# Two column tiles in one bank for the half-size group of the last layer's first product, and every other row store of the group before from GpSimd

## The chip, the core and the metric

The kernel runs on one core of one Trainium2 chip. The metric is the device time of one execution in microseconds (us); where several runs are given, it is their median. The program uses five engines that run side by side: PE (matrix products, with PEld for its weight loads), DVE (element-wise work, 32x32 transposes), ACT (copies and activations), POOL (GpSimd) and SP (which here issues DMAs). They wait for each other through semaphores. Products accumulate in PSUM banks of 128 partitions by 512 fp32 values.

## The reference

Three layers follow one another; all data are fp32.

```python
def reference(q, k, v, moe..., moe2...):
    x = attention(q, k, v)            # 8 batches x 8 heads, 576 rows, softmax inside chunks of 64
    x = x.reshape(4608, 512)
    x = ((x @ w1) * (x @ w2)) @ w3 @ w_out          # moe: 512 -> 1024 -> 512
    h = x @ w_in                                    # moe2: 512 -> 2048
    g = np.maximum(h, 0) + alpha * np.minimum(h, 0) # one alpha for each of the 2048 columns
    return g @ w_out2                               # 2048 -> 512
```

Only the last layer, moe2, is touched by the change.

## The kernel before

**Precision.** An fp32 operand is held as two parts, a rounded high part and the remainder. A product of two operands is three matmuls (PASSES: high·low, high·high, low·high), and a product over 256 values of the inner dimension is six matmuls ("x6" in the rows).

**moe2 in groups.** The 4608 tokens are nine blocks of 512 (TB). Both products of moe2 are computed in a Strassen-like way, as seven products of sums of quadrants in place of eight of the quadrants. Four groups (s = 0 to 3) take two blocks each; the fifth (s = 4) takes the one block left over and splits it in two halves of 256 tokens. That is `wide = [512, 512, 512, 512, 256]`: a matmul of a wide group has 512 columns, one of the half-size group 256.

**First product** (lines 595 to 651). The loop at line 610 goes over the groups and, in each, over the eight column tiles j of the hidden layer, two at a time (`jj`). One turn of that loop is called a pass here: four for each group, 20 in all. A pass has 14 steps of six matmuls: products 4 of both tiles into the banks `a` and `b`, product 5 of the first tile into one bank of a pair called `bc`, 3, 5, then 0, 2, 6 and 1. The pairs `bc` rotate over three places (`att`, `p01`, `p23`). ACT copies `a` and `b` after products 4, 3 and 0 into temporaries named p1, u2 and v (`keep`, L619; rows shorten the names to p, u, v); DVE adds the banks of `bc` to them (`add`, L441). `leaky` (L601 to L608) takes a finished quadrant: ACT forms relu(h) (L605, into a new tile `r`) and relu(-h) (L606), DVE joins the two with alpha (L607), and SP stores `r` to DRAM (L608, `g_dram<-r`). All the temporaries, r, t, p1, u2, v and the later `o` too, come from one pool of seven buffers of 128 x 512 fp32 (`tmp`, TMP = 7), also where only 256 columns are used. A buffer of `r` is free when its store has landed.

**Second product** (lines 724 to 800). Each group reads its quadrants back (`raw`, L678: `araw<-g_dram`, four slots, fetched three ahead on SP), splits them or their sums into two parts (`spread`: ACT casts at L658, DVE subtracts at L441), and multiplies. A group has three loops over m = 0 to 3; the first multiplies by two operands into the banks `a`, `b` and `q`, the second by three, the third by two. The results lie in a tile `post`. Those of a wide group are written out while the next group is in its first loop: `rows` (L710 to L721) is called eight times for a group; each call has DVE transpose 32x32 pieces of `post` into a tile `o` (L716) and then issues four stores of 64 KB (L720, `out<-o 32x4x128`), so 32 stores for a group. The half-size group, the last, has `turned` in its place (L696 to L708), which transposes on PE.

**What sets the order.** A scheduler puts the instructions of each engine in order; on PE the order of the code is kept through the whole of moe2. Each engine works through its queue in order, so an instruction that waits holds up all behind it on that engine. SP issues every DMA of the kernel before; POOL issues none. While the half-size group is in its first product, SP also fetches the second product's weights into places that come free (`weights`, L431).

Of the kernel before, what the change touches and what calls it, by code (L numbers as in the profile page):

```python
# [14 lines left out]
ALU = mybir.AluOpType  # L15
# [3 lines left out]
P = 128  # L19
TB = 512  # L20
# [47 lines left out]
def tile_attention_moe_moe(ctx: ExitStack, tc: tile.TileContext, qkv: bass.AP, w12: bass.AP,  # L68
# [54 lines left out]
    def tmp(name):  # L123
        return work.tile([P, TB], F32, tag="tmp", name=name, bufs=TMP)
# [9 lines left out]
    def bank(which):  # L134
        return psum.tile([P, TB], F32, tag=which, name=which, bufs=1)
# [459 lines left out]
    def product(s, j, o, ps, first, last):  # L595
# [3 lines left out]
                       start=first and k + i == 0, stop=k == 1 and i == 2, skip_group_check=not (first and last))  # L599
        if j == NJ - 1 and s + 1 < len(wide):  # L600
            operand(o)  # L601
    def leaky(s, j, q, h, t):
        w, f = wide[s], j + NJ * (q % 2)
        r = tmp("r")[:, :w]
        nc.scalar.activation(out=r, in_=h, func=AF.Relu)  # L605
        nc.scalar.activation(out=t, in_=h, func=AF.Relu, scale=-1.0)  # L606
        nc.vector.scalar_tensor_tensor(out=r, in0=t, scalar=nalpha[:, f:f + 1], in1=r, op0=ALU.mult, op1=ALU.add)  # L607
        nc.sync.dma_start(out=g2_dram[s, q, j // 2][:, j % 2], in_=r)  # L608

    for s, j in [(s, j) for s in range(len(wide)) for j in range(0, NJ, 2)]:  # L610
        w, jj = wide[s], (j, j + 1)
        if j == 2 and s + 1 < len(wide):
            load_y(s + 1)
        a = [bank(n)[:, :w] for n in "ab"]
        p1, u2, v, b, c = ([None] * 2 for _ in range(5))

        def keep(name, i):
            t = tmp(name)[:, :w]
            nc.scalar.copy(t, a[i])  # L619
            return t  # L620

        def second(i):
            n = 4 * NJ * s + j + i
            bc = pair(("att", "p01", "p23")[n % 3], "bc")
            b[i], c[i] = (bc[:, h, :w] for h in range(2))
            product(s, jj[i], 5, b[i], True, True)
            add(p1[i], p1[i], b[i])
            leaky(s, jj[i], 0, p1[i], p1[i])

        for i in range(2):  # L630
            product(s, jj[i], 4, a[i], True, False)
            p1[i] = keep("p1", i)
        second(0)
        for i in range(2):
            product(s, jj[i], 3, a[i], False, False)
            u2[i] = keep("u2", i)
        second(1)
        for i in range(2):
            product(s, jj[i], 0, a[i], False, False)
            v[i] = keep("v", i)  # L640
        for i in range(2):
            product(s, jj[i], 2, c[i], True, False)
            add(v[i], v[i], c[i])
            leaky(s, jj[i], 3, v[i], v[i])
        for i in range(2):
            product(s, jj[i], 6, a[i], False, True)
            leaky(s, jj[i], 1, a[i], tmp("t")[:, :w])
        for i in range(2):
            product(s, jj[i], 1, c[i], False, True)
            add(u2[i], u2[i], c[i])  # L650
            leaky(s, jj[i], 2, u2[i], u2[i])

# [57 lines left out]
    def rows(s, quads, half, t):  # L710

        w = wide[s]
        o = tmp("o")
        ob = o.rearrange("p (b h e c) -> p h e b c", b=4, h=2, e=2)
        for h, c in enumerate(quads):
            nc.vector.transpose(ob[:, h], c[:, :, t * P:(t + 1) * P].rearrange("p e (b c) -> p e b c", c=32))  # L716
        b, r = (PAIRS[s][half], 0) if w == TB else (0, half * w)
        r += b * TB + t * P
        for a in range(4):
            nc.sync.dma_start(out=out[r:r + P, a * P:(a + 1) * P].rearrange("(b r) c -> r b c", r=32),  # L720
                              in_=o[a * 32:(a + 1) * 32].rearrange("p (b c) -> p b c", c=P))  # L721

    x_t.pop("w")
# [124 lines left out]
```

## Time and profile before

| what | us |
|---|---|
| median of three runs | 1462.27 |
| lowest and highest of them | 1460.94 and 1463.52 |
| the profiled execution's own time | 1463.75 |
| its span, from the first to the last instruction | 1461.9 |
| PE busy in the span | 1411.9 |
| first product of moe2, four wide groups | 743.00 to 1054.98 |
| first product, half-size group | 1054.98 to 1105.42 |
| second product, four wide groups | 1105.42 to 1410.63 |
| second product, half-size group | 1410.63 to 1455.31 |

The stretches are cut where PE begins with a stage. The granted TensorE clock over the span was 0.995 of full speed. In the rows, a tile's name before the arrow is what is written, behind it what is read; "x6" is the number of instructions put together; "us" behind the start is their busy time. Matmuls overlap, so a group's busy time is longer than the time to the next group's start; the step from start to start is what counts.

### The profile page before, as it was taken

How to read it: one execution, taken by the hardware profiler on the slowest of the kernel's cores; microseconds unless marked ns; L12 is line 12 of the kernel's file. 1: busy time of each engine (PE TensorE's matmuls, PEld its weight loads, DVE VectorE, ACT ScalarE, POOL GpSimd, SP SyncE). 2: the span in 40 equal slices, each digit the busy share in tenths (PEclk: the TensorE clock that was granted, in tenths of full speed). 3: DMA queues.
4: the chain of work that ended last, by engine and by line, in shares of the span. 5: the costliest groups of instructions: out<-in, count | busy, mean ns of one | idle time of the engine just before them, and what ended most of it. 6: DMA issues, size and time to landing. Idle time of an engine off the chain costs nothing.

```text
span 1461.9 us, 22936 instructions
## 1 busy us (share of the span) xinstructions
PE 1411.9 (97%) x8608; PEld 1167.7 (80%) x8608; DVE 1001.7 (69%) x1533; ACT 737.5 (50%) x1603; POOL 0.7 (0%) x6
## 2 busy tenths in 40 slices
PE   4999999999999999999999999999999999999998
PEld 3777788887788888888878787878787888888887
DVE  4988786233487877776345758575756878888775
ACT  5545532144355545553247767686765444444433
POOL 0000000000000000000000000000000000000000
PEclk9999999999999999999999999999999999999999
DMA  8555342344466666668272424333589563745442
GB/s 260 188 188 168 108 157 95 131 151 148 141 216 217 216 216 220 218 221 304 91 273 108 148 112 158 116 137 116 177 277 324 188 216 116 210 136 176 144 140 89
DMA packets 132095, 256.32 MB, mean 175 GB/s; under 512 B 13712, under 2 KB 62864, under 8 KB 131984
## 3 DMA queue, kind: packets, MB, share of 16 engines
q1 hardware_dynamic: 131984, 254.87, 52.0%
q8 instruction: 67, 1.10, 0.3%
q14 instruction: 44, 0.36, 0.1%
HBM read 160.44 MB, written 94.37 MB: 174 GB/s over the span
## 4 chain that ended last, share of the span: by engine, by line
PE 83%; DVE 6%; ACT 5%; DMA 4%; issue 1%; SPq 0%; ACTq 0%; DVEq 0%
PE a L109 18%; PE b L109 18%; PE q L109 17%; PE acc L109 12%; PE bc L109 8%; PE ab L109 4%; PE wc L109 3%; ACT e L303 2%; DMA g_dram<-r 2%; PE sc L109 1%; PE pa L109 1%; DMA raw<-in_w 1%; PE pa L114 1%; DVE m L181 1%; DVE m L196 1%
## 5 line engine op out<-in xcount | busy, mean ns | idle before, releaser
L109 PE MATMUL q<-op,w 128*128 128x512 f32 (+1 forms) x1020 | 220.5, 369 | 2.2 <-DVE op L441 2.1
L109 PE MATMUL acc<-gs,wc 128*128 128x512 f32 x864 | 207.9, 393 | 3.4 <-DVE gs L121 3.1
L109 PEld LDWEIGHTS q<-op,w 128*128 128x128 f32 x1020 | 179.4, 190 | 34.4 <-DVE op L441 2.6
L109 PEld LDWEIGHTS acc<-gs,wc 128*128 128x128 f32 x864 | 160.3, 188 | 40.7 <-DVE gs L121 5.2
L109 PE MATMUL a<-x,wa 128*128 128x512 f32 x672 | 165.1, 394 | 0.4 <-DVE x L342 0.4
L109 PE MATMUL b<-x,wa 128*128 128x512 f32 x672 | 163.9, 392 | 0.0
L109 PEld LDWEIGHTS a<-x,wa 128*128 128x128 f32 x672 | 127.1, 190 | 27.1 <-DVE x L342 0.5
L109 PEld LDWEIGHTS b<-x,wa 128*128 128x128 f32 x672 | 124.8, 188 | 25.8
L109 PE MATMUL bc<-yo,w 128*128 128x512 f32 (+1 forms) x600 | 134.6, 368 | 0.0
L658 ACT CAST op<-araw 128x1024 fp32r<-128x1024 f32 (+1 forms) x80 | 77.3, 967 | 94.4 <-PE q L109 33.1
L109 PEld LDWEIGHTS bc<-yo,w 128*128 128x128 f32 x600 | 105.5, 189 | 18.7
L109 PE MATMUL b<-yo,w 128*128 128x512 f32 (+1 forms) x450 | 105.3, 369 | 1.7 <-ACT t L606 1.4
L441 DVE TENSOR_TENSOR op<-araw,op 128x1024 fp32r<-128x1024 f32 (+1 forms) x80 | 88.8, 1112 | 21.1 <-ACT op L658 20.5
L109 PE MATMUL ab<-x,wa 128*128 128x512 f32 x384 | 96.4, 400 | 4.9 <-ACT a L507 4.9
L109 PE MATMUL a<-yo,w 128*128 128x512 f32 (+1 forms) x390 | 92.1, 372 | 7.3 <-ACT p L619 5.0
L303 ACT ACTIVATE e<-sc,mx 128x64 f32<-128x64 f32 x288 | 86.2, 351 | 21.8 <-DVE mx L292 21.0
L109 PEld LDWEIGHTS b<-yo,w 128*128 128x128 f32 x450 | 79.1, 188 | 17.4 <-ACT t L606 3.0
L658 ACT CAST op<-sum 128x1024 fp32r<-128x1024 f32 (+1 forms) x60 | 58.0, 967 | 64.8 <-PE q L109 48.2
L109 PEld LDWEIGHTS ab<-x,wa 128*128 128x128 f32 x384 | 71.5, 190 | 23.2 <-ACT a L507 8.4
L109 PEld LDWEIGHTS a<-yo,w 128*128 128x128 f32 x390 | 68.3, 188 | 23.1 <-ACT p L619 6.6
L441 DVE TENSOR_TENSOR op<-sum,op 128x1024 fp32r<-128x1024 f32 (+1 forms) x60 | 66.6, 1109 | 28.1 <-ACT op L658 28.1
L303 ACT ACTIVATION_READ_ACCUMULATOR e<-sc,mx 128x1 f32 x288 | 70.1, 244 | 0.0
(121 smaller groups left out, 2075.6 us busy)
## 6 DMA issues: line engine op xcount, KB each, us to landing
araw<-g_dram SPq DMA_DIRECT2D x80, 512.0 KB, 3.9
g_dram<-r SPq DMA_DIRECT2D x128, 256.0 KB, 2.0
w_dram<-wm SPq DMA_DIRECT2D x48, 512.0 KB, 2.9
w<-w_dram SPq DMA_DIRECT2D x48, 512.0 KB, 4.9
qk<-in_qkv SPq DMA_DIRECT2D x36, 512.0 KB, 5.8
raw<-in_w2nd SPq DMA_DIRECT2D x32, 512.0 KB, 4.2
y_dram<-y SPq DMA_DIRECT2D x36, 256.0 KB, 2.8
raw<-in_w SPq DMA_DIRECT2D x16, 512.0 KB, 4.2
```

Source lines behind the costliest of these rows:

```text
L109: ins = nc.tensor.matmul(*args, **kw)
L114: ins = nc.tensor.transpose(*args, **kw)
L181: nc.vector.scalar_tensor_tensor(out=m.bitcast(U32), in0=conv_raw[i][:, :, 1], scalar=0xC0000000, in1=m.bitcast(U32), op0=ALU.bitwise_and, ...
L196: nc.vector.tensor_tensor(out=m, in0=m, in1=g[:, HI].bitcast(F32), op=ALU.subtract)
L303: nc.scalar.activation(out=e[:, j, a, h], in_=s[:, h2, n * D:(n + 1) * D], func=AF.Exp, bias=mx[:, h2, n:n + 1], scale=SCALE, accum_out=sm ...
L441: nc.vector.tensor_tensor(out=out, in0=x, in1=y, op=op)
L658: ins = nc.scalar.copy(out, x)
```

## The change

Two things are changed. The first is in the first product. Where a matmul has 256 columns, one bank of 512 now holds two column tiles side by side: the half-size group's eight column tiles are taken in two passes of four, two tiles to a bank, in place of four passes of two. Every step then is twelve matmuls (`both`), and each copy, addition and activation runs once over the 512 columns of two tiles; the joining with alpha, which has one alpha for each tile, still runs once for each tile over 256 columns, and a store moves both tiles (256 KB in place of 128). Only the first tile in a bank starts it. The pair `bc` is now chosen by the count of passes. The wide groups' code comes out as before.

The second is in `rows`: for the last wide group (s = 3), whose 32 row stores are issued during the half-size group's second product, two of each four stores are issued from POOL (`nc.gpsimd`) in place of SP.

```diff
-    def leaky(s, j, q, h, t):
-        w, f = wide[s], j + NJ * (q % 2)
-        r = tmp("r")[:, :w]
+    def leaky(s, js, q, h, t):
+        w, r = wide[s], tmp("r")[:, :h.shape[1]]
         nc.scalar.activation(out=r, in_=h, func=AF.Relu)
         nc.scalar.activation(out=t, in_=h, func=AF.Relu, scale=-1.0)
-        nc.vector.scalar_tensor_tensor(out=r, in0=t, scalar=nalpha[:, f:f + 1], in1=r, op0=ALU.mult, op1=ALU.add)
-        nc.sync.dma_start(out=g2_dram[s, q, j // 2][:, j % 2], in_=r)
-
-    for s, j in [(s, j) for s in range(len(wide)) for j in range(0, NJ, 2)]:
-        w, jj = wide[s], (j, j + 1)
+        for i, j in enumerate(js):
+            f, at = j + NJ * (q % 2), slice(i * w, (i + 1) * w)
+            nc.vector.scalar_tensor_tensor(out=r[:, at], in0=t[:, at], scalar=nalpha[:, f:f + 1], in1=r[:, at],
+                                           op0=ALU.mult, op1=ALU.add)
+        j = js[0]
+        to = g2_dram[s, q, j // 2]
+        nc.sync.dma_start(out=to[:, j % 2] if len(js) == 1 else to, in_=r if len(js) == 1 else r.rearrange("p (j c) -> p j c", j=2))
+
+    passes = []
+    for s, w in enumerate(wide):
+        n = TB // w
+        passes += [(s, j, [list(range(j + i * n, j + (i + 1) * n)) for i in range(2)]) for j in range(0, NJ, 2 * n)]
+
+    for turn, (s, j, jj) in enumerate(passes):
...
+        def both(i, o, ps, first, last):
+            w = wide[s]
+            for n, k in enumerate(jj[i]):
+                product(s, k, o, ps[:, n * w:(n + 1) * w], first and n == 0, last)
...
         def second(i):
-            n = 4 * NJ * s + j + i
-            bc = pair(("att", "p01", "p23")[n % 3], "bc")
-            b[i], c[i] = (bc[:, h, :w] for h in range(2))
-            product(s, jj[i], 5, b[i], True, True)
+            bc = pair(("att", "p01", "p23")[(2 * turn + i) % 3], "bc")
+            b[i], c[i] = (bc[:, h] for h in range(2))
+            both(i, 5, b[i], True, True)
             add(p1[i], p1[i], b[i])
             leaky(s, jj[i], 0, p1[i], p1[i])
 
         for i in range(2):
-            product(s, jj[i], 4, a[i], True, False)
+            both(i, 4, a[i], True, False)
             p1[i] = keep("p1", i)
...
         for a in range(4):
-            nc.sync.dma_start(out=out[r:r + P, a * P:(a + 1) * P].rearrange("(b r) c -> r b c", r=32),
+            queue = nc.gpsimd if s == len(PAIRS) - 1 and a % 2 else nc.sync
+            queue.dma_start(out=out[r:r + P, a * P:(a + 1) * P].rearrange("(b r) c -> r b c", r=32),
                               in_=o[a * 32:(a + 1) * 32].rearrange("p (b c) -> p b c", c=P))
```

Up to the half-size group's first pass the order on every engine is the same as before. PE's queue at the start of that pass, in the kernel before (`yo` is an operand of the group, `w_...` and `wx` weights):

```order
L109 MATMUL a<-yo,w_6802 128x256 x6
L109 MATMUL b<-yo,w_6880 128x256 x6
L109 MATMUL bc<-yo,w_6802 128x256 x6
L109 MATMUL a<-yo,w_6800 128x256 x6
L109 MATMUL b<-yo,w_6878 128x256 x6
L109 MATMUL bc<-yo,w_6880 128x256 x6
```

and in the changed kernel:

```order
L109 MATMUL a<-yo,w_6802 128x256 x6
L109 MATMUL a<-yo,w_6880 128x256 x6
L109 MATMUL b<-yo,w_7213 128x256 x6
L109 MATMUL b<-yo,wx 128x256 x6
L109 MATMUL bc<-yo,w_6802 128x256 x6
L109 MATMUL bc<-yo,w_6880 128x256 x6
L109 MATMUL a<-yo,w_6800 128x256 x6
L109 MATMUL a<-yo,w_6878 128x256 x6
```

The two tiles of one product now follow each other into the same bank, so PE meets the first bank `a` again after twelve matmuls more than before. The count of matmuls is the same.

SP's queue at the change from the fourth wide group to the half-size one in the second product, before (a load's name has quadrant and m: `g_dram_0_2` is the quadrant with index 0, m = 2):

```order
L720 DMA out<-o 32x4x128 x8
L678 DMA araw<-g_dram_3_2_251 128x2x256
L720 DMA out<-o 32x4x128 x8
L678 DMA araw<-g_dram_2_3_248 128x2x256
L678 DMA araw<-g_dram_3_3_252 128x2x256
L720 DMA out<-o 32x4x128 x8
L678 DMA araw<-g_dram_0_0_237 128x2x256
L678 DMA araw<-g_dram_2_0_245 128x2x256
L720 DMA out<-o 32x4x128 x8
L678 DMA araw<-g_dram_0_1_238 128x2x256
L678 DMA araw<-g_dram_2_1_246 128x2x256
L678 DMA araw<-g_dram_0_2_239 128x2x256
```

and now:

```order
L733 DMA out<-o 32x4x128 x4
L690 DMA araw<-g_dram_3_2_251 128x2x256
L733 DMA out<-o 32x4x128 x4
L690 DMA araw<-g_dram_2_3_248 128x2x256
L690 DMA araw<-g_dram_0_0_237 128x2x256
L690 DMA araw<-g_dram_3_3_252 128x2x256
L733 DMA out<-o 32x4x128 x4
L690 DMA araw<-g_dram_2_0_245 128x2x256
L733 DMA out<-o 32x4x128 x4
L690 DMA araw<-g_dram_0_1_238 128x2x256
L690 DMA araw<-g_dram_2_1_246 128x2x256
L690 DMA araw<-g_dram_0_2_239 128x2x256
```

Each block of eight stores is one of four, the loads keep their order but for `0_0`, which stands ahead of `3_3` now, and sixteen stores have gone from this queue. They stand on POOL's, behind the few instructions of its start:

```order
masks.py:197 MEMSET ident 128x128
masks.py:199 ISA
masks.py:199 AFFINE_SELECT ident<-ident 128x128
L733 DMA out<-o 32x4x128 x16
L858 UNCONDITIONAL_BRANCH
```

DVE's queue at the same place, before (`o_12891` is the last of the group's eight tiles `o`, and `post_10369<-q` the addition that closes the fourth group):

```order
L441 TENSOR_TENSOR sum_12798<-araw_12742,araw_12744 128x2x256
L441 TENSOR_TENSOR post_10369<-q_12102,post_10369 128x1024
L441 TENSOR_TENSOR op_12753<-sum_12746,op_12752 128x2x256
L716 STREAM_TRANSPOSE o_12832<-post_10369 128x2x4x32
L441 TENSOR_TENSOR op_12801<-araw_12744,op_12800 128x2x256
L716 STREAM_TRANSPOSE o_12839<-post_10369 128x2x4x32
L716 STREAM_TRANSPOSE o_12884<-post_10369 128x2x4x32
L441 TENSOR_TENSOR op_12805<-sum_12798,op_12804 128x2x256
L716 STREAM_TRANSPOSE o_12884<-post_10369 128x2x4x32
L716 STREAM_TRANSPOSE o_12891<-post_10369 128x2x4x32 x2
L441 TENSOR_TENSOR sum_12850<-araw_12794,araw_12796 128x2x256
```

and now (`o_12779` is the last of the eight):

```order
L728 STREAM_TRANSPOSE o_12727<-post_10257 128x2x4x32
L441 TENSOR_TENSOR op_12637<-araw_12578,op_12636 128x2x256
L728 STREAM_TRANSPOSE o_12772<-post_10257 128x2x4x32
L728 STREAM_TRANSPOSE o_12779<-post_10257 128x2x4x32
L441 TENSOR_TENSOR post_10257<-q_11990,post_10257 128x1024
L441 TENSOR_TENSOR op_12641<-sum_12634,op_12640 128x2x256
L728 STREAM_TRANSPOSE o_12720<-post_10257 128x2x4x32
L441 TENSOR_TENSOR op_12689<-araw_12632,op_12688 128x2x256
L728 STREAM_TRANSPOSE o_12727<-post_10257 128x2x4x32
L441 TENSOR_TENSOR sum_12738<-araw_12682,araw_12684 128x2x256
L441 TENSOR_TENSOR op_12693<-sum_12686,op_12692 128x2x256
L728 STREAM_TRANSPOSE o_12772<-post_10257 128x2x4x32
```

The first transpose into the eighth tile has moved ahead of the closing addition; with seven buffers, it waits until the four stores of the first tile, two from SP and two from POOL, have landed.

## Rows read from the trace of the kernel before

**Rows 1.** Windows: stretch, its length, engines' busy us (instructions), granted clock, DMA share, GB/s.

```profile
743.00:1054.98 311.98, 307.14 (x1345) 251.58 (x1344) 195.75 (x262) 225.25 (x379) 0.00 (x0) 1.00 0.39 142
1054.98:1105.42 50.44, 43.96 (x337) 40.98 (x335) 30.60 (x63) 33.89 (x91) 0.00 (x0) 1.00 0.85 279
1410.63:1455.31 44.68, 42.46 (x337) 41.99 (x336) 31.05 (x52) 17.23 (x30) 0.00 (x0) 0.96 0.40 112
1430.70:1434.30 3.60, 3.60 (x18) 3.60 (x19) 2.68 (x5) 0.68 (x2) 0.00 (x0) 0.56 0.50 135
1120.00:1130.00 10.00, 10.00 (x45) 8.26 (x45) 5.22 (x6) 5.17 (x7) 0.00 (x0) 1.00 1.01 399
```

**Rows 2.** PE timeline: start, us, matmuls; wide pass, half-size stage's start and its end.

```profile
1016.90 1.52 PE L109 MATMUL a<-yo,wx 128*128 128x512 f32 x6
1018.26 1.52 PE L109 MATMUL b<-yo,w 128*128 128x512 f32 x6
...
1055.69 0.88 PE L109 MATMUL b<-yo,w 128*128 128x256 f32 x6
1056.41 0.88 PE L109 MATMUL bc<-yo,w 128*128 128x256 f32 x6
1059.23 0.98 PE L109 MATMUL a<-yo,w 128*128 128x256 f32 x6 [1.94 <-ACT p L619]
...
1105.42 0.96 PE L109 MATMUL a<-op,w 128*128 128x512 f32 x3 [1.26 <-ACT t L606]
```

**Rows 3.** What PE waited for in the half-size stage: us in total, times, longest.

```profile
PE a L109 <- ACT p L619: 3.6, 4, 1.9
```

**Rows 4.** ACT by form: one wide pass and more, then the half-size stage.

```profile
L605 ACT ACTIVATE r<-p 128x512 f32<-128x512 f32 x4 | 2.5, 632 | 5.9 <-DVE p L441 5.9
...
L619 ACT COPY p<-a 128x512 f32<-128x512 f32 x2 | 1.2, 579 | 0.0
...
L619 ACT COPY p<-a 128x256 f32<-128x256 f32 x4 | 1.4, 351 | 0.0
```

**Rows 5.** Stores of the first product: the half-size stage's, then the wide passes'.

```profile
  ACT v L619: 3.1, 4
...
DMA to landing us min/median/max: 1.7/3.5/4.6
...
DMA to landing us min/median/max: 2.0/2.0/2.9
```

**Rows 6.** SP's queue before the load that was waited for; the chain's step on it.

```profile
1400.85 5.34 SPq L720 DMA_DIRECT2D out<-o  x8
...
1416.98 1.18 SPq L678 DMA_DIRECT2D araw<-g_dram  x2
1418.26 4.01 SPq L720 DMA_DIRECT2D out<-o  x8
...
1423.65 4.97 DMA araw<-g_dram
```

**Rows 7.** DVE around that load.

```profile
1428.64 0.69 DVE L441 TENSOR_TENSOR sum<-sum,araw 128x512 f32<-128x512 f32 x1 [1.22 <-DMA araw<-g_dram]
...
1429.96 0.68 DVE L441 TENSOR_TENSOR op<-araw,op 128x512 fp32r<-128x512 f32 x1
```

**Rows 8.** PE timeline of the same stretch.

```profile
1426.87 1.70 PE L109 MATMUL q<-op,w 128*128 128x256 f32 x12
1430.70 2.59 PE L109 MATMUL q<-op,w 128*128 128x256 f32 x12 [2.12 <-DVE op L441]
...
1435.16 1.12 PE L109 MATMUL q<-op,w 128*128 128x256 f32 x8
```

**Rows 9.** DVE while the last 32 row stores are issued.

```profile
L716 DVE STREAM_TRANSPOSE o<-post 128x256 f32<-128x256 f32 x16 | 6.1, 421 | 2.4 <-ACT post L658 2.4
```

**Rows 10.** Row stores: issue to landing over all 128; the last output stores.

```profile
DMA to landing us min/median/max: 1.6/2.4/5.7
...
1457.00 1.84 SPq L708 DMA_DIRECT2D out<-o  x4
```

More of the change, by code (lines that the diff above doesn't have):

```diff
@@ L601, in product @@
             operand(o)
-    def leaky(s, j, q, h, t):
-        w, f = wide[s], j + NJ * (q % 2)
-        r = tmp("r")[:, :w]
+    def leaky(s, js, q, h, t):
+        w, r = wide[s], tmp("r")[:, :h.shape[1]]
         nc.scalar.activation(out=r, in_=h, func=AF.Relu)
         nc.scalar.activation(out=t, in_=h, func=AF.Relu, scale=-1.0)
-        nc.vector.scalar_tensor_tensor(out=r, in0=t, scalar=nalpha[:, f:f + 1], in1=r, op0=ALU.mult, op1=ALU.add)
-        nc.sync.dma_start(out=g2_dram[s, q, j // 2][:, j % 2], in_=r)
-    for s, j in [(s, j) for s in range(len(wide)) for j in range(0, NJ, 2)]:
-        w, jj = wide[s], (j, j + 1)
+        for i, j in enumerate(js):
[10 more added lines that the diff above has]
+    for turn, (s, j, jj) in enumerate(passes):
         if j == 2 and s + 1 < len(wide):
             load_y(s + 1)
-        a = [bank(n)[:, :w] for n in "ab"]
+        a = [bank(n) for n in "ab"]
         p1, u2, v, b, c = ([None] * 2 for _ in range(5))
+        def both(i, o, ps, first, last):
+            w = wide[s]
+            for n, k in enumerate(jj[i]):
+                product(s, k, o, ps[:, n * w:(n + 1) * w], first and n == 0, last)
         def keep(name, i):
-            t = tmp(name)[:, :w]
+            t = tmp(name)
             nc.scalar.copy(t, a[i])
@@ L634, in tile_attention_moe_moe @@
         for i in range(2):
-            product(s, jj[i], 3, a[i], False, False)
+            both(i, 3, a[i], False, False)
             u2[i] = keep("u2", i)
@@ L638, in tile_attention_moe_moe @@
         for i in range(2):
-            product(s, jj[i], 0, a[i], False, False)
+            both(i, 0, a[i], False, False)
             v[i] = keep("v", i)
         for i in range(2):
-            product(s, jj[i], 2, c[i], True, False)
+            both(i, 2, c[i], True, False)
             add(v[i], v[i], c[i])
@@ L645, in tile_attention_moe_moe @@
         for i in range(2):
-            product(s, jj[i], 6, a[i], False, True)
-            leaky(s, jj[i], 1, a[i], tmp("t")[:, :w])
+            both(i, 6, a[i], False, True)
+            leaky(s, jj[i], 1, a[i], tmp("t"))
         for i in range(2):
-            product(s, jj[i], 1, c[i], False, True)
+            both(i, 1, c[i], False, True)
             add(u2[i], u2[i], c[i])
```

## The prediction

> **What bounds the kernel now.** I read the table of windows first, one window for each stage of the last layer [rows 1]. In the wide groups' first product PE is busy for 307.14 of 311.98 us: it is the bound, and only more or faster matmuls would change it. In the half-size group's it is busy for 43.96 of 50.44, with ACT at 33.89, DVE at 30.60 and the DMA engines at 0.85 of their time: no engine is full, so they wait for each other. The half-size group's second product has a smaller hole, 42.46 of 44.68 at a granted clock of 0.96. The change touches these two places and nothing else in PE's work.
>
> Then PE's timeline [rows 2], for the step that a stage would keep without waits. In a wide pass six matmuls start 1.36 us after the six before (1016.90 to 1018.26); in the half-size stage 0.72 us (1055.69 to 1056.41). Fourteen steps in four passes make 56 x 0.72 = 40.32 us, and the stage takes 50.44: it loses 10.12 us. The first loss is the longest: at 1056.41 + 0.72 = 1057.13 PE was free, and it went on at 1059.23, released by ACT's copy of bank `a`: 2.10 us. The last is at its end, 1.26 us for ACT again. The view of waits puts ACT's copy p first, with 3.6 us in four waits [rows 3], once in each pass; the rest are short ones.
>
> Why ACT is late: it has 22 operations in a pass (6 copies, 16 activations), and at 256 columns these don't get shorter by half. The copy takes 351 ns at 256 columns and 579 at 512 [rows 4]. On top, ACT waits for buffers: the half-size stage's stores land after 3.5 us in the median, up to 4.6, where the wide passes' take 2.0, and ACT's v alone waits 3.1 us for such a landing [rows 5].
>
> **Part 1, two tiles to a bank.** PE's count stays at 336 matmuls of 256 columns; 40.32 us remains the floor. ACT goes from 88 operations to 44 of 512 columns, at 579 to 632 ns [rows 4]: 22 x 0.61 = 13.4 us in a pass of 28 x 0.72 = 20.16, two thirds. Before, the same engine was busy for 33.89 of 50.44 us and PE's passes would have been 10.08. The pattern is now that of a wide pass, whose steps are 1.36 us where here they are 1.44, with the same ACT operations. So the wide groups are the model: 16 passes x 14 x 1.36 = 304.64 against 311.98 us, a loss of 0.46 a pass at most, mostly the cast of the next group's operands, which the half-size group doesn't have to make. DVE keeps 32 joinings of 256 columns and halves its 24 additions: it gets shorter, and PE waited for none of its work there. SP issues 16 stores for 32, with the same bytes.
>
> Two losses stay. At the start ACT is still busy with the wide pass before: its copy of `a` ended near 1059.23 and, 0.23 us longer now, ends near 1059.46, while PE comes back to `a` after six of the old steps, at 1054.98 + 4.32 = 1059.30. That is 0.2, say 0.3 with the hop between engines. At the end the second product's first matmul must wait for the last reading of bank `a` or `b`, and that waits for a buffer of which the store has to land; the last `t` is wanted at most some 0.7 us after the pass's last matmul and comes within half a us of it with landings of 3.5 us. I take 0.4. So part 1 gives 10.12 - 0.3 - 0.4 = 9.4 us. Bounds: 10.1 if nothing stays, and half, 5.1, if landings hold ACT as they do now.
>
> **Part 2, half the row stores from POOL.** Back from the hole [rows 8]: the twelve matmuls at 1426.87 take 12 x 0.12 = 1.44, so PE was free at 1428.31 and went on at 1430.70, after DVE's op: 2.39 us. That op ran from 1429.96 [rows 7], behind a sum that waited until 1428.64 for a load. The chain gives that load: issued at 1423.65, under way for 4.97 [rows 6]. It stands behind a block of eight stores that kept SP from 1418.26 for 4.01 us [rows 6], 0.50 each. The block now has four: 2.0 us earlier, and as much again from the block before it (which delayed two loads that this chain's DVE steps also wait for); of the load's own issue I can count on some 3 us, since then its slot comes free only when DVE has used up its former content. PE needs 2.39. So it lands in time, with some 0.6 to 1 us to spare.
>
> After the hole PE ran slowly: from 1430.70 to 1435.16 it made 24 matmuls, 4.46 us in place of 2.88, in a stretch at a granted clock of 0.56 [rows 1, 8], that is near the lower of the two levels, 1.2 GHz for 2.4. The clock had been 1.00 through the half-size stage with its waits of up to 1.94 us, so that the pause of 2.39 brought it down is likely, not shown. Without the pause I take both back: 2.39 + 1.58 = 3.97 us. Bounds: 0, if another thing comes last there, and with the whole of that stage's 44.68 - 40.32 = 4.36, 4.4. Below 0 SP can't bring it: its queue only gets shorter, and the one load that moved (`0_0`) moved ahead.
>
> What POOL takes for a store no row shows. The lower bound is SP's 0.50; the upper one is 5.7, the slowest landing of a row store [rows 10], if POOL were held until each has landed. It lies nearest to SP's issue, the same act on another engine: I take 1 us. It has cover. The first of these stores is ready at 1400.85 [rows 6], the last output of the kernel is issued by 1457.00 + 1.84 = 1458.84 [rows 10]: 58 us for 16 stores, 3.6 each, before they set the end. A shorter cover is DVE's: its first transpose into the eighth tile now waits for the first tile's stores, two of them POOL's, and stands ahead of the closing addition and of two operands of PE. DVE comes there about 1411, ten us after the first store; two stores and a landing of 2.4 fit in that up to 3.8 us each. So part 2 costs nothing there at 1 us.
>
> DVE in that stretch makes 16 transposes [rows 9]; its other work there is additions and subtractions. The Trainium skill, page "SBUF — State Buffer", section "SBUF: two separate sides", speaks against this part: a DMA issued from POOL has its descriptors written by GpSimd, which is locked out while DVE runs an operation in a two-port mode, and the next section tells of a transfer that took 3.1 us in place of 0.62 next to such copies. By that, as an estimate, 16 stores at 3.1 us make 50 us, inside the cover of 58, so the sum would be the same; no run here shows a DMA from POOL.
>
> **The sum.** 9.4 + 3.97 = 13.4 us. The profiled run took 1463.75 with 1461.9 of span; the changed kernel would take 1450.35 profiled, 1448.5 of span. Against the median of 1462.27: 1448.9.
>
> **The rivals.**
> A. Part 2 gives nothing: the load is issued earlier but its slot, or DVE's order before it, comes last in its place, and the hole stays. For it: the loads rotate through four slots, and the spare time is under 1 us. Against: the 4.97 us of landing was with 32 stores in one queue. 1462.27 - 9.4 = 1452.9.
> B. Part 1 gives half: ACT waits for landings instead of its own queue. For it: DMA at 0.85 of its time, and the same bytes, 50.44 us x 279 GB/s = 14.1 MB, would have to move in 41 us, at 343 GB/s; landings get longer. Against: 399 GB/s is reached from 1120 to 1130 [rows 1], and a buffer has twice the time until it is wanted. 1462.27 - 5.1 - 4.0 = 1453.2. A and B both: 1457.2.
> C. The stage ends earlier, but the second product's first groups then wait for their weights and loads, that come through DMA engines already full there (1.01 of their time from 1120 to 1130 [rows 1]); up to all of part 1 is given back: 1458.3. With part 2 lost too: 1462.3, no change.
> D, the slower side. POOL takes more than 3.6 us for a store, so that its sixteenth comes after all else. Slower than before it is from (58 + 13.4)/16 = 4.5 us on; at 5 us the end is 16 x 5 - 58 = 22 us later than my forecast: about 1471. The upper bound, 5.7, lies beyond that point; that SP issues the same store in 0.50 speaks against it. The lock of which the Trainium skill's page "SBUF — State Buffer" speaks is one way to such a price; the page's own figure of 3.1 us would not reach it.
>
> **How the numbers follow.** Chances: the forecast 0.50, A 0.19, B 0.14, A with B 0.03, C 0.04, C with part 2 lost 0.05, D 0.05. The forecast with no loss left in either place would be 1462.27 - 10.1 - 4.4 = 1447.8; a run's spread of 1.3 takes the low end to 1446.5. The high end takes in A, B and both: 1457.5. About 0.2%, 2.9 us, is what a measurement here can tell from no change. Faster by more: 0.50 + 0.19 + 0.14 + 0.03 + 0.04 = 0.90. Same: 0.05. Slower: 0.05.
>
> **What would show it.** In the changed kernel's windows the half-size stage would be some 41 us long with PE busy for nearly all of it, the only wait for ACT's copy p the first, and the second stage near 40.5 us at a clock of 1.00, with no wait for DVE's op. The load of quadrant 0, m = 2, is issued 13.0 us after PE's start with that stage now (1423.65 - 1410.63) and would be at some 10. POOL's row would show 16 DMAs that end well before the last outputs. Wrong I would be if ACT waits for landings of `r` as long as before, if PE waits for weights behind the stage, if DVE waits for a landing of `o`, or if POOL's stores stand at the end of the chain.

## The result, and the profile after

The changed kernel takes 1451.79 us in the median of four runs (1449.69 to 1451.98), the kernel before 1462.89 beside it. The ratio is 0.9919, with a 95% interval of 0.9904 to 0.9935: 11.8 us less, between 9.5 and 14.0. The two medians lie 11.1 us apart, inside that interval. That is faster, inside the range that was given (1446.5 to 1457.5), and 2.9 us above the time that was named. The profiled run of the changed kernel took 1451.96 us, with a span of 1450.2.

The windows of the changed kernel, cut where PE begins with a stage (the columns are those of [rows 1], with the engines in the order PE, PEld, DVE, ACT, POOL): the half-size group's first product, the second product of the four wide groups, and that of the half-size group.

```profile
1054.69:1096.39 41.70, 40.81 (x337) 40.40 (x336) 28.35 (x48) 28.10 (x48) 0.00 (x0) 1.00 0.91 312
1096.39:1402.23 305.84, 305.02 (x1346) 252.19 (x1345) 250.37 (x269) 132.05 (x136) 4.50 (x8) 1.00 0.56 185
1402.23:1443.23 41.00, 40.58 (x338) 40.37 (x337) 30.14 (x52) 17.21 (x30) 4.35 (x8) 1.00 0.38 110
```

Beside [rows 1]: the first has gone from 50.44 to 41.70 us, the third from 44.68 to 41.00 with the granted clock at 1.00 in place of 0.96. The second, 305.21 before, is 305.84, since the wait at the border of the two stages now lies behind the border. With 0.3 us that came ahead of the stage and 0.4 us lost behind it, the spans' difference is complete: -0.3 - 8.7 + 0.6 - 3.7 + 0.4 = -11.7.

PE's timeline in the first of these stretches, as in [rows 2], and the one wait of the last:

```profile
1057.56 1.60 PE L109 MATMUL bc<-yo,w 128*128 128x256 f32 x12
1059.86 1.69 PE L109 MATMUL a<-yo,w 128*128 128x256 f32 x12 [0.70 <-ACT p L632]
...
1080.46 0.98 PE L109 MATMUL a<-yo,wx 128*128 128x256 f32 x6 [0.20 <-ACT p L632]
...
1096.39 0.86 PE L109 MATMUL a<-op,w 128*128 128x512 f32 x3
1098.07 0.97 PE L109 MATMUL b<-op,w 128*128 128x512 f32 x3 [0.82 <-ACT t L605]
...
1431.61 3.86 PE L109 MATMUL q<-op,w 128*128 128x256 f32 x30 [0.42 <-DVE op L441]
```

Two passes are left in place of four, and the small waits inside the passes are gone. Three remain: 0.70 and 0.20 us for ACT's copy p at the starts of the passes, 0.82 for ACT's t at the end. From start to start the first costs 1059.86 - (1057.56 + 1.44) = 0.86, and the three together some 2.2 us, where the prediction had 0.7. In the last stage 0.42 us of waiting for DVE's op is left of the 2.12 in [rows 8].

### The profile page after: what moved, and what is told of

Same layout as the page of the kernel before. It is cut to its first block, busy times and chain, and to the rows that moved or that the text cites. A ratio compares the mean times of both kernels' runs of the same rounds, so it can differ in the third digit from the quotient of the medians.

```text
span 1450.2 us, 22825 instructions
## 1 busy us (share of the span) xinstructions
PE 1405.7 (97%) x8608; PEld 1164.4 (80%) x8608; DVE 999.1 (69%) x1521; ACT 730.8 (50%) x1559; POOL 9.6 (1%) x22
## 3 DMA queue, kind: packets, MB, share of 16 engines
q0 software_dynamic: 512, 1.05, 0.2%
## 4 chain that ended last, share of the span: by engine, by line
PE 81%; DVE 6%; ACT 6%; DMA 5%; issue 2%; ACTq 0%; SPq 0%; DVEq 0%
PE b L109 18%; PE a L109 17%; PE q L109 17%; PE acc L109 12%; PE bc L109 8%; PE ab L109 4%; PE wc L109 3%; ACT e L303 2%; DMA g_dram<-r 2%; DMA raw<-in_w 1%; PE sc L109 1%; PE pa L109 1%; PE pa L114 1%; DVE m L181 1%; DMA g<-g_dram 0%
```

## The experiments

All of them in one table. The stages are taken from windows like those above, in one profiled run of each kernel: the half-size group's first product (floor: 56 x 0.72 = 40.32 us), the wide groups' second product, the half-size group's second product (floor 40.32).

| kernel | median, us | ratio to before, 95% interval | first product, half-size | second, wide | second, half-size |
|---|---|---|---|---|---|
| before | 1462.9 to 1464.6 | 1 | 50.44 | 305.21 | 44.68 |
| changed | 1451.79 | 0.9919 (0.9904 to 0.9935) | 41.70 | 305.84 | 41.00 |
| changed, run again | 1451.18 | 0.9910 (0.9895 to 0.9925) | 42.22 | 306.08 | 40.41 |
| part 1 alone | 1454.17 | 0.9934 (0.9920 to 0.9949) | 40.61 | 304.67 | 44.97 |
| part 2 alone | 1460.05 | 0.9973 (0.9964 to 0.9982) | 51.11 | 305.22 | 40.31 |
| changed, stores of 128 KB | 1451.10 | 0.9913 (0.9896 to 0.9929) | 40.87 | 305.36 | 40.31 |
| changed, ACT at 256 columns | 1451.33 | 0.9915 (0.9898 to 0.9931) | 42.57 | 304.67 | 41.24 |
| changed, all those row stores from POOL | 1456.19 | 0.9949 (0.9929 to 0.9969) | 41.43 | 304.88 | 46.04 |
| changed, copies first and t in its bank | 1448.94 | 0.9906 (0.9891 to 0.9921) | 40.31 | 304.67 | 41.06 |
| before, four more buffers | 1459.85 | 0.9981 (0.9972 to 0.9991) | 47.10 | 305.17 | 42.85 |
| before, copies first | 1466.15 | 1.0013 (0.9998 to 1.0027) | 50.95 | 306.01 | 42.41 |
| before, seven more buffers | 1457.51 | 0.9961 (0.9942 to 0.9980) | 43.28 | 306.74 | 43.03 |
| before, seven more and copies first | 1457.48 | 0.9951 (0.9936 to 0.9966) | 44.12 | 308.86 | 44.48 |

The median of the kernel before moved between 1462.9 and 1464.6 from one set of runs to the next, so kernels of different sets are compared by their ratios. How far a stage moves from run to run is seen where its code is the same: the first column has 41.70 and 42.22 us for the changed kernel, 50.44 and 51.11 for the first product of before.

### Each part alone

```diff
-            queue = nc.gpsimd if s == len(PAIRS) - 1 and a % 2 else nc.sync
+            queue = nc.sync
```

> Two tiles to a bank as in the changed kernel, but all 32 row stores of the last wide group from SP. Theory (each part removes its own hole, and the two add up): the half-size group's first product stays near 41.7 us, the hole of some 2.1 us behind DVE's op and the slow clock behind it come back, and the time is 1451.8 + 3.7 = 1455.5 us. Rival (the new order of the first product shifts loads and stores against each other so that the hole would be gone without POOL): 1451.8 us, no wait of PE above 0.5 us in the last stage.

Its first and last stage, and PE's wait in the last:

```profile
1056.12:1096.73 40.61, 40.57 (x337) 40.37 (x336) 27.84 (x48) 28.13 (x48) 0.00 (x0) 1.00 0.91 320
1401.40:1446.37 44.97, 42.46 (x338) 41.98 (x337) 30.98 (x52) 17.02 (x30) 0.00 (x0) 0.96 0.37 108
...
1421.74 2.87 PE L109 MATMUL q<-op,w 128*128 128x256 f32 x12 [2.31 <-DVE op L441]
```

The hole is back, 2.31 us of waiting and a clock that is lower behind it (0.96 over the stage), and the ratio gives 0.9934 where the changed kernel has 0.9919. The intervals overlap; the stage, 44.97 against 41.00, is the better witness. The first stage loses only 0.3 us here, with the same queues on PE and ACT as in the changed kernel.

The other way round, the kernel before with the second part only:

```diff
-            nc.sync.dma_start(out=out[r:r + P, a * P:(a + 1) * P].rearrange("(b r) c -> r b c", r=32),
+            queue = nc.gpsimd if s == len(PAIRS) - 1 and a % 2 else nc.sync
+            queue.dma_start(out=out[r:r + P, a * P:(a + 1) * P].rearrange("(b r) c -> r b c", r=32),
```

> The kernel before with every other row store of the last wide group from POOL, the first product untouched. Theory: the half-size group's first product takes 50.4 us as before, its second product 41.0 in place of 44.7 with a granted clock of 1.00; 1462.9 - 3.7 = 1459.2 us. Rival (the load is late for another reason than the stores ahead of it on SP): 44.7 us again and 1462.9.

```profile
1056.78:1107.89 51.11, 43.12 (x337) 40.83 (x335) 30.77 (x63) 34.04 (x92) 0.00 (x0) 1.00 0.85 273
1413.11:1453.42 40.31, 40.31 (x337) 40.30 (x336) 30.07 (x51) 17.21 (x30) 4.34 (x8) 1.00 0.37 106
```

The last stage is at its floor, the first as slow as before. So the 32 stores on SP's queue made the hole, and part 2 removes it by itself: 0.9973, 3.9 us. Moving the stores also changed the place of one load and the order of DVE's transposes; no run here takes those apart from the shorter queue. Multiplied, the two parts give 0.9934 x 0.9973 = 0.9907, within the interval of the whole: they add up.

### What the first part's gain came from

The prediction put the loss of the stage down to ACT's many short operations first, and to waits for buffers second. The first of these was put to the test by giving the operations back, with everything else as changed:

```diff
-        nc.scalar.activation(out=r, in_=h, func=AF.Relu)
-        nc.scalar.activation(out=t, in_=h, func=AF.Relu, scale=-1.0)
         for i, j in enumerate(js):
             f, at = j + NJ * (q % 2), slice(i * w, (i + 1) * w)
+            nc.scalar.activation(out=r[:, at], in_=h[:, at], func=AF.Relu)
+            nc.scalar.activation(out=t[:, at], in_=h[:, at], func=AF.Relu, scale=-1.0)
...
-            nc.scalar.copy(t, a[i])
+            for n in range(TB // wide[s]):
+                at = slice(n * wide[s], (n + 1) * wide[s])
+                nc.scalar.copy(t[:, at], a[i][:, at])
```

> The changed kernel with the same banks, passes and stores, but ACT's copies and activations of the half-size group made in two halves of 256 columns, so 88 operations again. Theory (the cost of many short operations on ACT made the loss of before): ACT is busy for 33 to 35 us of the stage, the first copy of a pass is late again, the stage takes 44 to 46 us and the kernel 1454 to 1456. Rival (twice as many matmuls between two uses of a bank is what helped, and ACT's count of operations matters little): the stage stays at 41.7 to 42.2 and the time at 1451.8 to 1452.3.

The stage's window, and PE's first wait in it (us in total, times, longest):

```profile
1056.38:1098.95 42.57, 40.86 (x337) 40.45 (x336) 28.66 (x49) 30.58 (x89) 0.00 (x0) 1.00 0.90 312
...
PE a L109 <- ACT p L634: 1.7, 2, 1.1
```

The rival was nearer. ACT has its 88 operations again, but PE lost only 42.57 - 40.32 = 2.25 us, where the changed kernel lost 1.4 inside the stage and the kernel before 10.1; the time did not move. So with banks of two tiles the count of ACT's operations costs at most 1 or 2 us; what it costs in the kernel before, this run alone does not show.

Then the buffers. In the kernel before a pass of 10.08 us takes sixteen temporaries out of seven buffers, so that one may be held for 10.08 x 7 / 16 = 4.4 us (an estimate from the step in [rows 2] and the buffers' count, and a mean over all tiles of the pass). A tile r is held for two activations of 0.42 us, the joining of 0.48 and a landing of 3.5 [rows 5]: 4.8 us, longer than that. In a wide pass the same sum gives 8.3 us for 4.0 that are needed, and in the changed kernel 8.8 us for 0.6 + 0.6 + 2 x 0.48 + 4.7 = 6.9, although its stores land later than before. The tiles r, half of all, are the only ones counted so; u is held for much longer, in the changed kernel from the copy at 1062.33 to beyond 1078, without PE waiting inside the pass, so that this is a rough measure. If that is what bound the stage, more buffers must help the kernel before, at its own steps of 0.72 us and with its 88 operations. Four more, for the tiles r of the first three passes:

```diff
-        r = tmp("r")[:, :w]
+        if w < TB and j < NJ - 2:
+            r = granule((18, 19, 20, 21)[spare[0] % 4], "r", F32)[:, 0, :w]
+            spare[0] += 1
+        else:
+            r = tmp("r")[:, :w]
```

> The kernel before with four more buffers for r in the first three of the half-size group's four passes (eleven in place of seven); banks, matmuls, the 88 operations on ACT and the row stores stay. Theory (in a pass of 10 us sixteen temporaries go through seven buffers, and a store keeps its buffer until it lands 3.5 us later: buffers made most of the loss): ACT's waits for landings fall from 7.6 us to under 3, the stage from 50.4 to 43 to 46 us, 1456 to 1459 us. Rival (steps of 0.72 us are too short for the handing over between PE, ACT and DVE, whatever the buffers): the stage stays above 48 us, 1461 to 1463.

```profile
1056.95:1104.05 47.10, 42.39 (x337) 40.73 (x335) 29.95 (x62) 33.28 (x92) 0.00 (x0) 1.00 0.85 281
...
ACT r L611 <- DMA g_dram<-r: 6.9, 7, 1.9
...
1060.98 0.97 PE L109 MATMUL a<-yo,w 128*128 128x256 f32 x6 [1.72 <-ACT p L625]
```

47.10 us: between the two expectations. The second line is ACT's wait for landings: it did not go away (in the kernel before it is 6.8 in all), since the eight tiles r of a pass now went through four buffers, 10.08 x 4 / 8 = 5.0 us each, about what one is held for. So seven, by the places 17, 15 and 16 besides:

> The kernel before with seven more buffers for r in the first three of the half-size group's passes, in place of four (fourteen in all). With four the stage fell from 50.4 to 47.1 us, and ACT still waited 6.9 us for landings. Theory (too few buffers for the landings made most of the loss): ACT's waits for landings go under 2 us and the stage to 43 to 45 us, 1456 to 1458. Rival (steps of 0.72 us are too short for the handing over between PE, ACT and DVE): the landings' waits go, but others take their place, and the stage stays at 46 to 48 us, 1459 to 1461.

The window, and PE's only two waits in it:

```profile
1056.06:1099.34 43.28, 41.02 (x337) 40.41 (x335) 27.82 (x60) 31.13 (x89) 0.00 (x0) 1.00 0.90 295
...
1092.18 0.98 PE L109 MATMUL a<-yo,w 128*128 128x256 f32 x6 [1.33 <-ACT u L625]
...
1099.34 0.96 PE L109 MATMUL a<-op,w 128*128 128x512 f32 x3 [0.93 <-ACT t L612]
```

The theory held: 43.28 us. The first three passes, that have fourteen buffers, end at 1056.06 + 3 x 10.08 = 1086.3, and up to there PE does not wait at all; both waits lie in the fourth pass, which has the old seven. In the kernel before, the passes after the first begin here, and the stage ends at 1105.42:

```profile
1068.54 0.98 PE L109 MATMUL a<-yo,w 128*128 128x256 f32 x6 [0.18 <-ACT t L606]
...
1080.20 0.98 PE L109 MATMUL a<-yo,wx 128*128 128x256 f32 x6 [0.24 <-ACT t L606]
...
1091.96 0.98 PE L109 MATMUL a<-yo,w 128*128 128x256 f32 x6 [0.26 <-ACT t L606]
```

From these starts its passes take 13.56, 11.66, 11.76 and 13.46 us, a loss of 3.5, 1.6, 1.7 and 3.4 against 10.08. With the seven more buffers the first three lose 0.1 in all and the fourth, which got none, 2.9. So 7.2 of the 10.1 us went. The second and third pass show it best: 22 operations a pass and steps of 0.72 us are as before, and 3.3 us of 3.3 are gone. For the first pass the buffers are not shown to be the cause alone, 2.1 us of it being the hole at the start. The new buffers are places in which the second product's first operands are made, so that two casts, 2.1 us of ACT's time ahead of the first copy p in the kernel before, had to come later. With four more buffers those casts were gone from there too and the hole stayed, with 1.72 us of waiting (the last line shown for them); what removed it with seven is open. (The casts then come late for the second product, which loses 1.5 us, so that this is no better kernel than the changed one.)

ACT's order by itself was changed in two ways. In the kernel before, the first two copies of each narrow pass were put ahead of the last activations of the pass before:

```diff
             p1[i] = keep("p1", i)
+        for args in late:
+            leaky(*args)
+        late = []
...
-            leaky(s, jj[i], 2, u2[i], u2[i])
+            if s == len(wide) - 1 and j < NJ - 2 or s == len(wide) - 2 and j == NJ - 2:
+                late.append((s, jj[i], 2, u2[i], u2[i]))
+            else:
+                leaky(s, jj[i], 2, u2[i], u2[i])
```

> The kernel before with one thing moved on ACT: the first two copies of each narrow pass are made before the last activations of the pass before. Theory (the copy p, first in the view of waits, is late since it stands behind activations): the waits for the copy p fall from 3.6 to under 1 us and the stage from 50.4 to 46 to 47.5, 1459 to 1460 us. Rival (ACT is late with all of its work since it waits for buffers, and a copy that comes earlier makes another later): the waits move to t, u and v, and the stage stays above 49 us, 1461.5 to 1463.

```profile
1054.29:1105.24 50.95, 44.36 (x338) 42.31 (x336) 31.32 (x64) 34.46 (x91) 0.00 (x0) 0.97 0.83 275
...
PE a L109 <- ACT u L620: 3.4, 3, 2.6
PE a L109 <- ACT t L606: 1.8, 2, 1.3
```

The waits for the copy p are gone and others have come, for u and t, one of them of 2.60 us: 50.95 us, no gain, and 1466.15 us for the kernel, above both expectations. The copy p stood first in the view of waits [rows 3] only because it was the next thing that PE needed when ACT was late. With the seven buffers the same move gave nothing either:

> The same seven more buffers and, besides, the first two copies of each narrow pass made before the last activations of the pass before. Theory (with buffers to spare, what is left of the loss is the copy p behind activations in ACT's queue): the stage falls to 41 to 43 us, 1454.5 to 1456.5. Rival (the handing over at steps of 0.72 us): as with the seven buffers alone, within 1 us.

The stage took 44.12 us and the kernel 1457.48, as with the buffers alone within the scatter. PE no longer waited for p, but 1.15 us for the copy u in the first pass.

### What is left in the changed kernel

The waits of the first profile could have been chance, since the same queues lost 0.3 us with all stores on SP. The changed kernel was run again:

> The changed kernel once more, unchanged, for a second look at its waits. If the waits of its first profile are its own (copy p 0.7 and 0.2, t 0.8 us), they come again and the half-size group's first product takes 41.5 to 41.9 us. If they differ from run to run, as the same queues with all row stores on SP (40.6 us) suggest, it takes between 40.5 and 41.7. Time 1451.8 within 1 us either way.

```profile
PE a L109 <- ACT p L632: 1.1, 1, 1.1
PE b L109 <- ACT t L605: 1.1, 1, 1.1
```

They came again, 1.1 us each, the short one at the second pass did not, and the stage took 42.22 us, above both expectations. So the two long waits are in both profiles of this kernel, and in the one with all stores on SP, whose PE and ACT have the same queues here, they are not; what makes the difference is open. ACT's timeline in the first profile of the changed kernel shows what they are, at the start of the stage and at its end; the first line is the same copy in the kernel before:

```profile
1058.83 0.35 ACT L619 COPY p<-a 128x256 f32<-128x256 f32 x1
...
1055.80 1.05 ACT L670 CAST op<-sum 128x1024 fp32r<-128x1024 f32 x1 [0.27 <-DVE sum L441]
1057.00 1.29 ACT L604 ACTIVATE r<-u 128x512 f32<-128x512 f32 x2 [0.16 <-DVE u L441]
1058.20 1.14 ACT L605 ACTIVATE u<-u 128x512 f32<-128x512 f32 x2
1059.24 0.57 ACT L632 COPY p<-a 128x512 f32<-128x512 f32 x1
...
1097.42 0.60 ACT L605 ACTIVATE t<-b 128x512 f32<-128x512 f32 x1 [2.10 <-DMA g_dram<-r]
```

The copy p of bank `a`, which PE had finished at about 1056.1, is made at 1059.24, behind a cast of the second product's first operand (1.05 us) and four activations of the wide pass before. That is no earlier than in the kernel before. The hole at the start is smaller, 0.86 us for 2.10, because PE comes back to `a` after 36 matmuls in place of 18, 4.32 us into the stage in place of 2.16: 1.2 us of the gain are due to this and not to buffers. At the end t waits 2.10 us for a buffer whose store has not landed. These stores land later than before ([rows 5]: 3.5 us):

```profile
  ACT r L604: 2.6, 1
...
DMA to landing us min/median/max: 2.1/4.7/5.9
```

The first of these lines is one more wait of ACT's for a landing, 2.6 us ahead of the second pass, behind which PE lost 0.35 us. Why the landings take longer is not shown: the stores are twice as large and the stage moves 312 GB/s for 279, but with all row stores on SP it moved 320 and they landed after 4.0.

Whether the stores' doubled size has a part in that was tried with 128 KB for each, two to a tile:

```diff
-        j = js[0]
-        to = g2_dram[s, q, j // 2]
-        nc.sync.dma_start(out=to[:, j % 2] if len(js) == 1 else to, in_=r if len(js) == 1 else r.rearrange("p (j c) -> p j c", j=2))
+        for i, j in enumerate(js):
+            nc.sync.dma_start(out=g2_dram[s, q, j // 2][:, j % 2], in_=r[:, i * w:(i + 1) * w])
```

> The changed kernel, but each of the half-size group's stores of 256 KB in the first product split into two of 128 KB, as many as in the kernel before (32). Theory (the end of the stage waits for a landing since the DMA engines are nearly full, whatever the store's size): PE's wait for t at the stage's end stays near 0.8 us and the time within 0.5 us of 1451.8. Rival (the landing of 4.7 us in the median comes from the doubled size): the landings go back to some 3.5 us, the wait at the end is gone, 1451.0.

```profile
1054.89:1095.76 40.87, 40.56 (x337) 40.35 (x336) 27.08 (x47) 28.36 (x49) 0.00 (x0) 1.00 0.89 301
```

No wait at the end in this run, landings of 4.2 us in the median, and 1451.10 us. As the wait at the end is missing in two kernels with the larger stores too (part 1 alone, and ACT at 256 columns), this does not tell the two theories apart: it stays open.

Both waits can be taken away by other means, the copies first as above and the last pass's t written over its own bank:

```diff
-            leaky(s, jj[i], 1, a[i], tmp("t"))
+            leaky(s, jj[i], 1, a[i], a[i] if turn == len(passes) - 1 else tmp("t"))
```

> The changed kernel with the two remaining waits of the half-size group's first product taken away: ACT makes the first two copies of a narrow pass before the last activations of the pass before, and the last pass's t is written over its bank in place of a temporary, so that it needs no buffer. Theory (the copies stand behind activations in ACT's queue, and t waits for a landing): no wait of PE above 0.3 us in the stage, 40.4 to 40.8 us, and 1451.8 - 1.2 to - 2 = 1450 us. Rival (the waits of the changed kernel differ from run to run by a us, whatever the order, as the stage of 40.6 us with all stores on SP suggests): within 0.5 us of 1451.1.

```profile
1053.88:1094.19 40.31, 40.31 (x337) 40.30 (x336) 28.46 (x50) 27.84 (x48) 0.00 (x0) 1.00 0.92 328
1094.19:1398.86 304.67, 304.67 (x1346) 252.26 (x1345) 249.93 (x268) 131.68 (x135) 4.48 (x8) 1.00 0.56 185
1398.86:1439.92 41.06, 40.57 (x337) 40.36 (x336) 30.00 (x51) 17.21 (x30) 4.34 (x8) 1.00 0.35 105
```

The stage is at its floor, 40.31 us, and the second product of the wide groups at its own, 4 x 76.16 = 304.64. The move of the copies did nothing in the kernel before, and here PE no longer waits for p; that this is because buffers hold ACT less is likely, not shown, since both moves were made at once. This is the fastest kernel of all, 1448.94 us; by the intervals (0.9891 to 0.9921) it can't be told from the changed one, while the two stages together show 2.6 us.

### All row stores from POOL

```diff
-            queue = nc.gpsimd if s == len(PAIRS) - 1 and a % 2 else nc.sync
+            queue = nc.gpsimd if s == len(PAIRS) - 1 else nc.sync
```

> The changed kernel with all four of each four row stores of the last wide group from POOL, none from SP (32 at 0.56 us are 18 us of POOL's time). Theory (the cover of some 50 us behind the stores hides POOL's price, and SP's queue is free enough with half of the stores gone): the last stage between 40.3 and 41.0 us as with half of them, 1451.8 us or up to 0.7 less. Rival (POOL becomes late: DVE waits for landings of the tiles o): PE waits in the last stage's first loop, 1453 to 1456.

PE's wait in the last stage, DVE's two operations ahead of its release, and POOL's last stores:

```profile
1420.42 1.01 PE L109 MATMUL a<-op,w 128*128 128x256 f32 x3 [2.82 <-DVE op L441]
...
1419.07 0.69 DVE L441 TENSOR_TENSOR araw<-araw 128x512 f32<-128x512 f32 x1 [2.40 <-DMA araw<-g_dram]
1419.68 0.69 DVE L441 TENSOR_TENSOR op<-sum,op 128x512 fp32r<-128x512 f32 x1
...
1405.96 8.64 POOL L733 DMA_DIRECT2D out<-o  x16 [3.08 <-DVE o L728]
```

It is slower than the changed kernel, by about the rival's size but not for its reason. POOL ends its 32 stores at 1414.6, and none of DVE's operations waits for a landing of `o`. What PE waited for is `op<-sum`, and that stands in DVE's queue behind a subtraction that waited 2.40 us for a load; in the changed kernel it stands ahead of that subtraction. The scheduler put the two the other way round; that it did so because it expected the load earlier without stores on SP is a guess. The load itself was issued at 1414.33, right behind DVE's last reading of its slot (1413.61 + 0.68), so a shorter queue on SP could not bring it earlier.

## Why the prediction was right, and where not

**The place and the sign** were right for both parts: the stage with no engine full, and the hole behind one load. The wide passes as the model of the new pass held too: inside the passes PE no longer waits. The model had more to tell. Two of the three rows of PE's waits in the wide groups' first product before are these, all at the change from one group to the next:

```profile
PE a L109 <- ACT p L619: 2.1, 2, 1.1
PE b L109 <- ACT t L606: 1.4, 3, 0.8
```

A copy p that is late by up to 1.1 us and a t by up to 0.8 are of the kind and near the size that the changed kernel kept at its borders.

**Part 1** was taken at 9.4 us and gave 50.44 - 41.70 - 0.63 = 8.1 in the first profile and 7.4 in the second; with all stores on SP it gave 10.4. The step that was mis-sized is the one on what stays: 0.3 at the start and 0.4 at the end, against some 0.9 and 1.0, and 0.35 at the second pass's start. At the start the working compared ACT's copy of before, 0.23 us longer, with PE's old step, and took ACT's queue as it was; the copy of the changed kernel began 0.4 us later than in the kernel before, in a stage that began 0.3 us earlier. At the end it took landings of 3.5 us, and they went to 4.7. That the landings would get longer stood under rival B; its size, half of the gain, did not come. ACT still waited 4.7 us for landings, of 6.8 before, but little of that reached PE.

**The reason for part 1** was only half right. ACT's 22 operations in a pass, with a price that does not halve with the columns, were put first. They are true and cost little: given back, they took at most 1 or 2 us, and with more buffers the second and third pass ran without waits next to all of them. The waits for buffers, put second, were the main thing: 7.2 of 10.1 us went with seven more buffers, though the 2.1 at the start are not shown to be theirs. The size came out right in part by luck: the change halves ACT's operations, doubles the time in which a buffer can be held and brings PE back to a bank later, all at once, so it did not matter which of them was the cause.

**Part 2** was taken at 3.97 us and gave 3.7 in the first profile of the changed kernel, 4.4 in that of part 2 alone, 3.9 by the ratio. The step of the issue was near too. SP's last block and the load:

```profile
1407.62 2.04 SPq L733 DMA_DIRECT2D out<-o  x4
...
L690 SPq DMA_DIRECT2D araw<-g_dram x1: 518/518/518, 1411.7 to 1411.7; - x1
...
DMA to landing us min/median/max: 3.6/3.6/3.6
```

Four stores take 2.04 us for 4.01 [rows 6]. The load was issued at 1411.68, 9.45 us after the stage's start, where it was 13.0 and some 10 was expected, and landed 3.6 us later, for 4.97 before. The hole is not of one size: the runs with 32 stores on SP lost between 2.1 and 4.7 us in the last stage.

**POOL's price** was taken at 1 us, between 0.50 and 5.7, and is 0.56, next to SP's own:

```profile
L733 POOL DMA_DIRECT2D out<-o x16 | 8.9, 559 | 1399.9 <-DVE o L728 1399.9
...
out<-o POOLq DMA_DIRECT2D x16, 64.0 KB, 3.1
...
out<-o SPq DMA_DIRECT2D x16, 64.0 KB, 3.3
```

POOL's stores land after 3.1 us in the median, and the sixteen that SP issues in the same stretch after 3.3; the 2.4 of [rows 10] is the median over all groups. Rival D had no place. The Trainium skill's lock, page "SBUF — State Buffer", section "SBUF: two separate sides", did not show: the sixteen issues took 0.55 to 0.68 us each while DVE ran transposes, additions and subtractions next to them. The section tells of a DVE operation in a two-port mode, with an fp32 copy within SBUF as its example; no such copy ran in that stretch, so that no run here tests that case.

**Rival A** did not come true in the changed kernel, but it is close behind: with all stores off SP the slots, and DVE's order, were what came last, and 0.42 us of waiting is left with half of them. **Rival C** did not come: the second product began without waits for loads or weights.

The time of the sum, 1448.9, needs both parts at their full size; the shortfall against the median, 1451.8, is the 1.3 to 2 us of part 1's remaining waits, some 0.3 of part 2's, 0.4 behind the last stage, and the scatter of the runs.

## What to carry to other kernels

Where no engine is full and PE waits for copies, count buffers before operations: the time of a pass, times the buffers, divided by the tiles that it takes, should be longer than a tile is held in the mean, with its store's landing. It is a rough measure, since tiles are held for unequal times. The view of waits names the operation that PE needed next, not the one that made the engine late: moving it alone only moved the wait, in the kernel before and with seven more buffers too; in the changed kernel it helped. A few stores ahead of a load in a queue can make it late enough to stop PE; here taking half of them away was enough, and with all taken away the scheduler put a waiting operation ahead of one that was needed.

## What was not expected of the hardware

The low clock does not go by the length of one pause alone. PE's waits of up to 1.94 us left it at 1.00; after 2.12 us [rows 8], after 2.31 with part 1 alone and after 2.82 with all stores from POOL it was near one half. But a wait of 2.23 us, in the first product of the kernel with part 2 alone, was followed by six matmuls in 0.97 us, at full speed. PE's timeline there:

```profile
1061.32 0.97 PE L109 MATMUL a<-yo,w 128*128 128x256 f32 x6 [2.23 <-ACT p L619]
```

The same view of the kernel before with its copies first, and the window behind that pause:

```profile
1061.35 1.52 PE L109 MATMUL a<-yo,w 128*128 128x256 f32 x6 [2.60 <-ACT u L620]
...
1061.35:1065.80 4.45, 4.45 (x24) 4.45 (x25) 1.44 (x4) 1.80 (x5) 0.00 (x0) 0.62 0.92 316
```

And the window behind the pause of 2.82 us, with all row stores of that group from POOL:

```profile
1420.42:1424.00 3.58, 3.58 (x16) 3.58 (x17) 1.75 (x3) 0.61 (x1) 0.00 (x0) 0.50 0.46 126
```

There six matmuls took 1.52 us after 2.60, and the granted clock was 0.62 over 4.45 us, or 0.50 over 3.58: the lower level of 1.2 GHz for part or all of the stretch. What decides it stays open. Where the clock falls, the hole costs well over its pause: in [rows 8] 1.58 us on top of 2.39 from start to start. That the pause brought the clock down fits each fall shown here, and no run shows it by itself.
